# Regrouped tokens, a subtraction moved to TensorE, one pool of 21 tiles and new orders in a recurrence-and-experts kernel

## The chip, the cores and the metric

The kernel runs on one core of one Trainium2 chip. The metric is the device time of one execution in microseconds; the median of three runs of the kernel before is 293.84 us (289.77, 293.84 and 294.34). TensorE (PE) multiplies matrices, VectorE (DVE), ScalarE (ACT) and GpSimd (POOL) work elementwise, SyncE (SP) issues nearly all DMAs.

## The reference

The input is four sequences of 5056 tokens with 256 channels, 20224 tokens in all, everything fp32. First a gated linear recurrence runs along each sequence, then a soft mixture of 8 experts with 4 slots each (32 slots) runs over all tokens:

```
a_t = exp(8 * sigmoid(r) * log(sigmoid(a_param)))
h   = a_t * h + sqrt(max(1 - a_t*a_t, 1e-6)) * sigmoid(i) * x     # y[:, t] = h
logits = y @ phi                                                  # 20224 x 32
d = softmax of logits over the tokens;  slots = d.T @ y           # 32 x 256
slot_out = relu(slots @ w1[e]) @ w2[e]                            # per expert, 256 -> 1024 -> 256
out = softmax of logits over the slots @ slot_out
```

The experts need a maximum and a sum over all tokens, so no output row can be written before the last token has passed the recurrence.

## The kernel before, in words

Tokens are cut into 40 quads of 512 (the last has 256), and quads into 21 units: quad 0, then pairs of quads (1024 tokens), then quad 39. Tasks carry names: a letter code, a number (quad, unit or group) and often the half of the channels after a dot.

Per quad or unit, before the experts:

- `Dr`, `Di`, `Dx` load the three inputs (512 KB each). `TR` transposes r on PE into a two-bank tile of PSUM (tag `pair`, of which there are three), `SR` takes a tanh of it on ACT (L835) into a tile `A`, `EX` an exp (L912, two units in one instruction where their tiles are neighbours).
- `SQ` squares `A` on POOL (L896), `RT` takes the root on ACT (L931), `SI` is the gate of i on ACT (L850 or L848), `P1` (L864, L866) turns a tanh into a sigmoid, `U` multiplies gate and x on POOL (L876). A letter per unit in the string `IV` chooses the gate: P has the `P1`, E lets PE add i*x and x while it transposes (twice the transposes in `TU`, L950, no `P1`), S uses the sigmoid table.
- `TU` transposes the product into a `pair` tile (L950); on DVE `ST` (L967) multiplies it by the root there and `SC` (L984) scans it, 1024 tokens per instruction.
- `TY` (L1010) transposes the scan's result back, `YC` copies it to a tile `yn` on DVE (L1026) or ACT (L1024), in halves of 512 columns, each through half a `pair` or a single-bank tile (tag `one`, of which there are two).

Tokens are gathered into groups: 1536 tokens in the first, 2048 in the next nine, 256 in the last. Per group `LG` computes logits (L1090), `LE` copies them and takes a running maximum M on DVE (L1103), `LD` forms M minus logits on POOL (L1133; the last two groups on DVE, L1137), `TE` transposes that, `ES` takes the exp (L1157), `AC` multiplies by `yn` (L1179), `DD` and `DM` form the factor that rescales the sum (L1164, L1167), and `AE` adds on DVE (L1200). The last two groups share one maximum.

The end chain: `MT MX MR MC WJ WE W` find a maximum over the rows, `SP` contracts the sums with W (L1390), `SL` copies (L1400), `L1` and `L2` are the experts (L1439, L1487), `HZ` clears their operand on ACT (L1418), `HS`, `HT`, `HR` stand between, `SO`, `RS`, `SH` (L1503, L1505, L1508) copy, spread and copy the result. Then per group `CT CM CS CE RR CN` make the second softmax, `HP HE OT OE` (L1594, L1605, L1607, L1622, L1636, L1638) make outputs, and `OD` writes them (L1653). The weights (`w1e`, `w2e`: 16 transfers of two parts, L1342 and L1344) take freed input tiles.

Nothing chooses the order at run time: the constant `ORDER` names every task of each engine, and `run_fixed` replays it with durations only to give tiles out. PE gets spare transposes (`WU`, L1318) where that replay sees a gap. Each engine runs its own list in order and waits for what a task needs. Big tiles have tag `b`: 20 of [128, 2, 512], handed out by `take`; input tiles of one quad have tag `st`, five of them. Lines quoted here are those of the kernel before:

```
A[p - 1].mate = A[p]                 # second unit of an EX pair gets the neighbour tile
yp = Buf("pair" if q in YP4 else ONE, f"yp{q}.{b0}")      # YP4 = () before
```

Of the kernel before, what the change touches and what calls it, by code (L numbers as in the profile page):

```python
# [94 lines left out]
ORDER = {
    "PE": """
        AT TR0 TR1 TR2 TR3 TU0.1 TU0.0 TR5 TU1.0 TR6 TR4 TU1.1 TR7 TR9 TY0.0 TY2.0 TY0.2 TR10 TR8 TY1.0 LG0.0 LG0.1 TU2.0 TR11 TU2.1 TY1.2 TU3.1 TR12
        TU3.0 TR15 TY4.0 TR13 TR16 TY2.2 TR14 TY3.0 LG1.0 TY4.2 LG1.1 TU4.1 TE1 TE0 TU4.0 TR17 TR18 TU5.0 AC0.0 AC0.1 TY3.2 TU5.1 AC0.2 AC0.3 TY6.0
        TY5.0 TY8.0 TY7.0 CT1 TY8.2 TY6.2 TY5.2 AC1.0 AC1.1 AC1.2 AC1.3 TY7.2 TY9.0 TY9.2 TU6.0 TU6.1 LG2.0 TR19 LG2.1 TU7.0 TY10.0 TR21 TR22 TU7.1
        TR20 TU8.0 CT0 TR24 LG3.0 TR23 LG3.1 TY10.2 TU8.1 TR25 TR26 TE2 TY11.0 TU9.0 AC2.0 AC2.1 AC2.2 AC2.3 TE3 TY11.2 TY13.0 TU9.1 CT2 TR28 TY12.0  # L100
        TY15.0 TY14.0 TY13.2 TY14.2 TY16.0 TY12.2 TU10.1 TY16.2 TU10.0 LG4.0 AC3.0 LG4.1 TR27 AC3.1 AC3.2 AC3.3 TU11.0 TY17.0 TR29 TR30 TY18.0 TU11.1
        TY15.2 TR31 LG5.0 TU12.0 TR33 LG5.1 TU12.1 TR32 TR34 TY17.2 TU13.0 TE4 TY18.2 TU13.1 TE5 AC4.0 TY20.0 AC4.1 TR37 AC4.2 AC4.3 TY19.0 TY20.2
        TY23.0 TY24.0 TY21.0 TY22.0 TY22.2 TY19.2 TY21.2 TU14.1 LG6.0 TU14.0 LG6.1 TY23.2 TR35 TU15.0 AC5.0 AC5.1 TU15.1 AC5.2 AC5.3 TR38 TY25.0 TR36
        TY27.0 TU16.1 TY26.0 TE6 TU16.0 LG7.0 LG7.1 TU17.0 TR39 TY27.2 TY26.2 TY24.2 TY25.2 TY28.0 TU17.1 TE7 TY28.2 AC6.0 AC6.1 AC6.2 AC6.3 TY29.0
        TY29.2 TU18.1 TY31.0 TY31.2 TY30.0 TY30.2 TU18.0 LG8.0 AC7.0 AC7.1 LG8.1 AC7.2 AC7.3 TY32.0 TY33.0 TU19.0 TY34.0 TY33.2 TU19.1 TE8 TY32.2
        TY35.0 TY34.2 TY36.0 TU20.0 TY36.2 AC8.0 AC8.1 AC8.2 LG9.0 AC8.3 TU20.1 TY35.2 LG9.1 LG10.0 LG10.1 TY37.0 TY37.1 TY38.0 MT TY38.1 TE10 TE9
        TY39.0 TY39.1 MC AC9.0 AC9.1 AC9.2 AC9.3 AC10.0 CT4 SP DN L1.0 L1.1 L1.2 L1.3 L1.4 L1.5 L1.6 HT0 L1.7 L2.0 L2.1 L2.2 HT1 L2.3 L2.4 L2.5 L2.6
        L2.7 CT3 RS HP0.0 HP0.4 OT0.0 OT0.4 HP1.0 HP1.8 OT1.0 HP2.0 OT1.8 OT2.0 CT7 HP2.8 OT2.8 HP3.0 CT5 HP4.8 CT6 CT8 OT3.0 HP4.0 OT4.8 CT9 HP7.8
        HP3.8 OT4.0 CT10 OT7.8 OT3.8 HP5.8 HP6.8 HP7.0 OT5.8 OT7.0 HP6.0 HP5.0 HP8.0 OT6.0 OT6.8 OT8.0 OT5.0 HP9.0 HP9.8 HP8.8 OT9.0 OT8.8 HP10.0
        OT10.0 OT9.8  # L110
    """,
    "ACT": """
        SA LN SR0 EX0.1 EX0.0 SR1 SR2 SI0 EX1.0 EX1.1 SI1 RT0.0 RT1.0 SR3 SR5 SI3 SR6 SR4 EX2.0 SR7 SR9 EX2.1 SI5 SR8 SR10 RT2.0 RT3.0 SR11 EX4.0
        EX4.1 SR12 SI9 SR15 SI7 SR13 RT4.0 RT5.0 SR14 SR16 EX6.0 ES0 SR17 SR18 EX6.1 ES1 DM1 EX8.0 EX8.1 SI11 SI13 SI15 SI17 RT6.0 RT8.0 RT9.0 RT7.0
        SR19 SR21 SI23 SR22 SR20 DM2 EX10.0 EX10.1 SR23 SR24 SI19 SR25 SR26 ES2 YC11.0 EX12.1 EX12.0 ES3 YC11.2 SI21 YC12.0 RT10.0 YC16.0 RT12.0
        RT11.0 YC16.2 RT13.0 DM3 SR27 SR28 SI25 SR29 CE1 YC17.0 YC18.0 SR30 YC15.2 SR31 EX14.0 SR33 EX14.1 DM4 SR32 SR34 YC17.2 EX16.0 EX16.1 ES4 ES5
        SI27 SI29 RT15.0 RT14.0 RT17.0 SI31 SR35 SR37 SI33 RT16.0 SR38 SR36 YC27.0 DM5 EX18.0 EX18.1 YC26.0 ES6 SI35 YC27.2 SR39 YC26.2 YC24.2 SI37
        ES7 DM6 YC28.2 RT18.0 YC29.0 YC29.2 YC31.0 YC31.2 SQ19.1 YC30.2 YC30.0 RT19.0 CE2 YC32.0 YC33.0 DM7 EX20.0 YC34.0 SI39 EX20.1 YC33.2 ES8
        YC32.2 YC35.0 YC34.2 YC36.0 RT20.0 YC36.2 DM8 YC35.2 HZ YC37.0 YC37.1 YC38.0 YC38.1 ES9 YC39.0 ES10 WE YC39.1 DM9 CE4 HS0 HS1 CE0 HE0.0 HE0.4
        OE0.0 OE0.2 OE0.4 HE1.0 OE0.7 CE3 HE2.0 OE1.2 OE1.1 OE1.8 OE1.11 OE1.9 HE2.8 OE2.8 OE2.2 OE2.9 CE7 OE2.10 HE4.8 OE2.11 OE3.0 OE3.1 OE3.3 CE5  # L120
        CE6 OE4.8 OE4.10 HE3.8 OE4.1 OE4.2 OE4.3 OE7.8 OE7.11 OE7.10 OE7.9 OE3.9 CE9 HE5.8 CE8 OE3.11 HE7.0 OE5.8 OE5.10 HE6.8 OE5.9 OE7.3 HE6.0 OE7.1
        OE6.0 CE10 OE6.2 OE6.1 OE6.3 OE6.8 OE6.11 OE5.2 OE8.1 OE5.1 HE9.8 OE8.8 OE9.2 HE10.0 OE8.9 OE9.3 OE10.0 OE9.8 OE8.11
# [1567 lines left out]
```

## Time and profile before

| | us |
|---|---|
| median of three runs | 293.84 |
| the runs | 289.77, 293.84, 294.34 |
| span of the profiled execution, first to last instruction | 287.8 |
| fastest run, 2.0 above that span | 289.77 |
| busy: PE, ACT, DVE, POOL | 249.0, 241.4, 230.1, 195.7 |
| moved by DMA | 100.04 MB |
| written to the output | 20.71 MB |

The profile has no separate time for its own execution; the span is 2.0 us under the fastest of the three runs. Busy time is an average over stages: the recurrence lasts until about 207 us, the experts to 231 us, and from 237 us the outputs are written. The share of one stage is read from the views by window.

### The profile page before, as it was taken

To read this page: it belongs to the slowest core of one execution; us is meant where nothing else is said; L and a number is where in the kernel's file an instruction comes from. 1 tells how busy PE (TensorE), PEld (TensorE's weight loads), DVE (VectorE), ACT (ScalarE), POOL (GpSimd) and SP (SyncE) were. 2 spreads that over 40 slices of the span, in tenths; PEclk is the share of its full clock that TensorE was granted. 3 is DMA by queue.
4 is the path that set the end of the run, shared out by engine and by line. 5 is a ranking of instruction groups with operands and counts; after the bars stand their busy time and mean duration, and the time that the engine had idled before them with its cause. 6 is when DMAs were issued, how large, how long until landed. Compare 5 with 4: busy or idle time off the path is not lost.

```text
span 287.8 us, 6063 instructions
## 1 busy us (share of the span) xinstructions
PE 249.0 (87%) x2359; PEld 186.6 (65%) x2359; DVE 230.1 (80%) x280; ACT 241.4 (84%) x265; POOL 195.7 (68%) x152
## 2 busy tenths in 40 slices
...
POOL 1399997989999999999999999997102201132000
...
GB/s 280 415 408 410 401 409 410 406 409 406 408 380 232 277 381 294 317 186 223 380 412 318 364 299 369 370 370 335 360 416 361 9 110 419 416 414 416 419 410 283
DMA packets 27408, 100.04 MB, mean 348 GB/s; under 512 B 3058, under 2 KB 3060, under 8 KB 24948
## 3 DMA queue, kind: packets, MB, share of 16 engines
...
q14 instruction: 10, 0.08, 0.1%
HBM read 78.94 MB, written 20.71 MB: 346 GB/s over the span
## 4 chain that ended last, share of the span: by engine, by line
PE 29%; ACT 24%; DMA 12%; DVE 11%; POOL 11%; issue 8%; SPq 1%; DVEq 0%; ACTq 0%; POOLq 0%
DMA b<-in_i_gate_dram 7%; PE bank L1622 6%; POOL b L876 6%; ACT b L835 5%; DVE b L984 5%; ACT b L912 4%; ACT b L931 4%; PE pair L950 3%; ACT b L848 3%; PE bank L1439 3%; DMA st<-in_moe_w_dram 3%; PE bank L1487 2%; DVE pair L967 2%; DMA b<-in_x_dram 2%; ACT b L850 2%
## 5 line engine op out<-in xcount | busy, mean ns | idle before, releaser
L876 POOL TENSOR_TENSOR b<-b,b 128x1024 f32<-128x1024 f32 x36 | 84.9, 2386 | 0.2
L896 POOL TENSOR_TENSOR b<-b 128x1024 f32<-128x1024 f32 (+2 forms) x40 | 72.7, 1839 | 13.8 <-ACT b L912 10.7
L950 PE MATMUL pair<-ident,b 128*128 128x128 f32 x412 | 52.9, 276 | 7.9 <-ACT b L835 4.2
L950 PEld LDWEIGHTS pair<-ident,b 128*128 128x128 f32 x412 | 45.0, 141 | 17.8 <-POOL b L876 7.7
L967 DVE SCALAR_TENSOR_TENSOR pair<-b,pair 128x1024 f32<-128x1024 f32 (+2 forms) x42 | 48.2, 1149 | 8.2 <-PE pair L950 4.9
L984 DVE TENSOR_TENSOR_SCAN b<-b,pair 128x1024 f32<-128x1024 f32 (+6 forms) x26 | 47.6, 1845 | 0.2
L984 DVE TENSOR_TENSOR_SCAN b<-b,b,pair 128x1024 f32<-128x1024 f32 (+2 forms) x22 | 45.6, 2076 | 0.4
L824 PE MATMUL pair<-ident,st 128*128 128x128 f32 x316 | 41.8, 280 | 4.2 <-DVE b L984 1.5
L912 ACT ACTIVATE b<-b,ca 128x2048 f32<-128x2048 f32 (+3 forms) x24 | 42.2, 1798 | 0.1
L824 PEld LDWEIGHTS pair<-ident,st 128*128 128x128 f32 x316 | 35.4, 143 | 10.7 <-DVE b L984 5.1
L1557 POOL TENSOR_TENSOR b<-b,rs_all 128x512 f32<-128x512 f32 (+2 forms) x11 | 10.5, 961 | 46.1 <-DVE rs_all L1552 20.3
L835 ACT ACTIVATE b<-pair 128x1024 f32<-128x1024 f32 (+1 forms) x40 | 39.1, 1013 | 2.4 <-PE pair L824 2.3
L1010 PE MATMUL one<-ident,b 128*128 128x128 f32 x200 | 31.1, 280 | 4.0 <-ACT yn L1024 1.2
L1622 PE MATMUL bank<-hs,hT 32*128 32x256 f32 x234 | 27.8, 420 | 4.1 <-DVE hT L1607 1.9
L1010 PEld LDWEIGHTS one<-ident,b 128*128 128x128 f32 x200 | 22.0, 141 | 11.9 <-DVE yn L1026 3.8
L1636 ACT COPY b<-bank 128x512 f32<-128x512 f32 x36 | 20.0, 597 | 10.3 <-PE bank L1622 9.5
L931 ACT ACTIVATE b<-b 128x2048 f32<-128x2048 f32 (+2 forms) x15 | 25.9, 1768 | 0.1
L1622 PEld LDWEIGHTS bank<-hs,hT 32*128 32x128 f32 x234 | 18.6, 197 | 9.3 <-DVE hT L1607 3.1
L1622 PE MATMUL one<-hs,hT 32*128 32x256 f32 x82 | 21.2, 430 | 1.9 <-ACT hT L1605 1.1
L1026 DVE COPY yn<-one 128x512 f32<-128x512 f32 x29 | 19.5, 681 | 2.6 <-PE one L1010 2.6
L850 ACT ACTIVATE b<-b 128x2048 f32<-128x2048 f32 x11 | 21.1, 1921 | 0.0
L1090 PE MATMUL one<-b,phi_sb 128*32 128x512 f32 x156 | 20.9, 601 | 0.1
...
## 6 DMA issues: line engine op xcount, KB each, us to landing
...
```

The source lines that it names most:

```text
L824: nc.tensor.transpose(out=o[:, m, :], in_=raw("r", q)[:, m * D + h * P : m * D + (h + 1) * P], identity=ident,)
L835: nc.scalar.activation(dst, t(rp)[:, :, :c], AF.Sigmoid if SIGR else AF.Tanh, scale=1.0 if SIGR else 0.5)
L850: nc.scalar.activation(v, v, AF.Tanh, scale=0.5)
L876: eng.tensor_tensor(out=o, in0=a, in1=b, op=ALU.mult)
L896: eng.tensor_tensor(out=o, in0=v, in1=v, op=ALU.mult)
L912: nc.scalar.activation(v, v, AF.Exp, scale=ca[:, h : h + 1], bias=ca[:, h : h + 1])
L931: nc.scalar.activation(v, v, AF.Sqrt, bias=quarter if f != 1.0 else f, scale=-f)
L950: nc.tensor.matmul(o[:, m, :], raw(nm, q)[:, m * D + h * P : m * D + (h + 1) * P], ident, is_transpose=True, start=(nm == nms[0] and m == ...
L967: nc.vector.scalar_tensor_tensor(v, t(Nb[p])[:, h, :c], 0.5e-3 if gate_of(quads(p)[0]) == "E" else 1e-3, v, op0=ALU.max, op1=ALU.mult)
L984: nc.vector.tensor_tensor_scan(dst, dst, flat()[:, s0:s1], init, op0=ALU.mult, op1=ALU.add)
L1010: nc.tensor.transpose(out=flat()[:, b * D + h * P : b * D + (h + 1) * P], in_=tokens(q, b0 + b, 1)(h), identity=ident,)
L1622: nc.tensor.matmul(t(ops[x])[:, c * D : (c + 1) * D], t(hT)[r, off : off + (P - 1) * ns + 1 : ns], t(soRb)[r, :], start=True, stop=True,)
```

## The change

- `GROUPING` becomes "B": the first group is quad 0 alone (512 tokens), eight groups of 2048 follow, then a group of 1024 tokens in four segments of 256, and the tail of 256: twelve groups, and the two that share the last maximum hold 1280 tokens instead of 2304.
- In groups 0 to 7 `LD` on POOL goes: `TE` transposes the logits themselves, and `TF` adds the negated maximum with four more transposes into the same bank; `NM` makes the negated maximum (five on POOL, three on DVE). Groups 8 to 11 keep `LD` (8, 10 and 11 on DVE, 9 on POOL), now in `st` tiles. `DD` goes: `DM` takes M before as bias.
- `YP4` lists nearly all quads: their `TY` fills one whole `pair` tile and one `YC` copies 1024 columns. `YC` moves from 43 DVE and 37 ACT instructions to 25 and 19.
- `IV` changes from PPEEEESSSSEPPESSSSPPP to PEEEEPEESSSSEPEPSSSPS: eight units of kind E instead of six.
- One SBUF tile holds 21 `b` tiles; `EX` takes two units at any distance up to 15 tiles. The separate tiles of `lD`, `hs` and `hT` go.
- r of quad 0 is loaded, transposed and passed in halves (`TR0`, `TR0b`, `SR0`, `SR0b`). `SQ0.1` and `P10` move from DVE to POOL, `P12` goes.
- The last `AE`, `SP`, `SO`, `RS` and `SH` are cut in two halves of columns. `HZ` moves from before the last copies to between the experts' two layers on ACT.
- All five lists of `ORDER` are new.

```diff
-        groups = [[(0, o, P) for o in range(0, QT, P)]]
+        groups = [[(0, 0, QT)]]
...
-        A[p - 1].mate = A[p]
-        A[p].led = True
+        A[p].near = A[p - 1]
...
+            lo, hi = sorted(A[u].slot[0] for u in (us if len(us) == 2 else us * 2))
+            if len(us) == 2 and hi - lo > 15:
+                vs = [t(A[u])[:, h, : plen(u)] for u in us]
             else:
+                vs = [T["all"][:, H * lo + h : H * hi + h + 1 : H * (hi - lo), :] if len(us) == 2 else t(A[p])[:, h, :c]]
...
+                    nc.tensor.matmul(
+                        t(ep)[:, b * rows : (b + 1) * rows],
+                        nM[:rows, mg : mg + 1].broadcast_to([rows, P]) if part else lS(g)[:rows, b * P : (b + 1) * P],
+                        ident[:rows, :rows], is_transpose=True, start=(part == 0 and b == 0), stop=(part == 1),
+                        skip_group_check=True,
+                    )
...
+            LD[g] = add(("POOL", "DVE"), f"LD{g}", 0.1 + 0.56 * L / QT, deps=[le], prio=pos - 30 + fin, emit=e_ld,
+                        alloc=[lD], uses=[lSb[g // 4]], alt={"DVE": 0.09 + 0.36 * L / QT})
...
-                nc.gpsimd.tensor_tensor(out=dm[:rows, g : g + 1], in0=M[:rows, g - 1 : g], in1=M[:rows, g : g + 1], op=ALU.subtract)
+                    dm[:rows, g : g + 1], M[:rows, g : g + 1], AF.Exp, scale=-1.0, bias=M[:rows, g - 1 : g])
...
+        for k, c in enumerate((slice(0, P), slice(P, D + 1))):
+                nc.vector.scalar_tensor_tensor(
+                    accS[:r, c], accS[:r, c], dm[:r, mg : mg + 1], t(acc)[:r, c], op0=ALU.mult, op1=ALU.add,
...
+        a = add("PE", "SP0", 0.26, deps=[w, AE["a"]], prio=-60, alloc=[sp], emit=lambda: e_sp(0), shape="M")
+        a = add("PE", "SP1", 0.26, deps=[a, AE["b"]], prio=-60, uses=[sp], emit=lambda: e_sp(1), shape="M")
```

The tail of the new orders, after the scan of unit 19 has begun (ACT and DVE):

```
ACT  YC29.0 YC30.0 YC29.2 RT20.0 YC31.0 SQ19.1 YC32.0 RT19.0 YC34.0 ES8 CE2 YC33.0 DM8 ES9 DM9 YC35.0 YC37.0
     YC38.0 YC36.0 DM10 YC38.1 ES10 CE1 ES11 YC39.1 WE CE4 HS0 CE3 HZ HS1 SO0 HE0.0 SH0 SH1
DVE  ST18.0 LD8 SC18.0 ST18.1 SC18.1 ST19.0 LE9 SC19.0 ST19.1 AE8 SC19.1 ST20.1 SC20.1 ST20.0 SC20.0 LE10 LE11 LD11
     AE9 MX LD10 MR YC37.1 WJ YC39.0 W AE11a AE11b CM4 SL
```

## Rows read from the trace of the kernel before

**Rows 1.** Page, part 2: POOL busy tenths and DMA rate in 40 slices of the span.

```profile
POOL 1399997989999999999999999997102201132000
...
GB/s 280 415 408 410 401 409 410 406 409 406 408 380 232 277 381 294 317 186 223 380 412 318 364 299 369 370 370 335 360 416 361 9 110 419 416 414 416 419 410 283
```

**Rows 2.** Stretches: us; busy (instructions) of PE, PEld, DVE, ACT, POOL; clock; DMA share; GB/s.

```profile
40.00:80.00 40.00, 34.78 (x297) 27.94 (x299) 35.86 (x34) 39.88 (x30) 36.64 (x21) 1.00 1.03 408
...
120.00:160.00 40.00, 38.17 (x348) 28.58 (x346) 39.53 (x39) 39.88 (x35) 39.74 (x25) 1.00 0.82 310
160.00:208.00 48.00, 43.40 (x421) 30.57 (x421) 47.83 (x44) 47.62 (x58) 40.11 (x29) 1.00 0.97 354
```

**Rows 3.** DVE timeline: start us, us, instruction, count, idle before; units 2, 19, 20.

```profile
40.27 1.23 DVE L967 SCALAR_TENSOR_TENSOR pair<-b,pair 128x1024 f32<-128x1024 f32 x1 [2.47 <-ACT b L931]
...
198.01 1.23 DVE L967 SCALAR_TENSOR_TENSOR pair<-b,pair 128x1024 f32<-128x1024 f32 x1
...
206.85 0.75 DVE L984 TENSOR_TENSOR_SCAN b<-b,b,pair 128x256 f32<-128x256 f32 x1
```

**Rows 4.** DVE timeline: pairs of equal instructions back to back.

```profile
54.78 1.26 DVE L1026 COPY yn<-one 128x512 f32<-128x512 f32 x2
...
85.83 2.36 DVE L967 SCALAR_TENSOR_TENSOR pair<-b,pair 128x1024 f32<-128x1024 f32 x2 [0.83 <-ACT b L931]
88.10 4.58 DVE L984 TENSOR_TENSOR_SCAN b<-b,b,pair 128x1024 f32<-128x1024 f32 x2
```

**Rows 5.** ACT timeline: a table load, copies, two tanh, the root of unit 19.

```profile
34.99 1.93 ACT L835 ACTIVATE b<-pair 128x1024 f32<-128x1024 f32 x2
...
185.81 1.28 ACT L931 ACT_TABLE_LOAD   x1
...
189.87 1.08 ACT L1024 COPY yn<-one 128x512 f32<-128x512 f32 x2
...
192.72 1.96 ACT L931 ACTIVATE b<-b 128x2048 f32<-128x2048 f32 x1
```

**Rows 6.** Groups by form, POOL: count, then busy us, mean ns, idle before.

```profile
L1133 POOL TENSOR_SCALAR lD<-b,M 128x512 f32<-128x512 f32 x8 | 5.6, 705 | 1.3 <-DVE b L1103 1.3
...
L1164 POOL TENSOR_TENSOR dm<-M 128x1 f32<-128x1 f32 x9 | 1.8, 213 | 6.5 <-DVE b L1103 6.5
```

**Rows 7.** Timeline, start of the run: one operation twice on DVE, and POOL beside it.

```profile
11.57 0.69 DVE L864 TENSOR_SCALAR st<-st 128x1024 f32<-128x1024 f32 x1 [2.82 <-ACT st L850]
...
15.64 2.38 DVE L864 TENSOR_SCALAR b<-b 128x1024 f32<-128x1024 f32 x1
...
12.74 4.73 POOL L896 TENSOR_TENSOR b<-b 128x1024 f32<-128x1024 f32 x2 [2.81 <-ACT b L912]
```

**Rows 8.** PE timeline: sixteen transposes, and the task after them.

```profile
37.47 1.91 PE L950 MATMUL pair<-ident,b 128*128 128x128 f32 x16
39.22 0.38 PE L1318 MATMUL one<-ident 128*128 128x128 f32 x2
```

**Rows 9.** Stretches as in rows 2, PE's spare transposes alone (PE, PEld).

```profile
40.00:80.00 40.00, 1.50 (x9) 0.66 (x7) 1.00 1.03 408
```

**Rows 10.** Timelines of ACT, PE, DVE and SP in the end chain.

```profile
207.20 1.91 ACT L1418 ACTIVATE b<-ident 128x2048 f32<-128x2048 f32 x1
...
211.81 2.37 PE L1179 MATMUL bank<-yn,eS 128*32 128x257 f32 x36
...
216.05 6.25 PE L1439 MATMUL bank<-b,yn 128*32 128x256 f32 x112 [0.39 <-DVE yn L1400]
...
231.29 0.42 DVE L1503 COPY hs<-bank 128x256 f32<-128x256 f32 x1 [2.21 <-PE bank L1487]
...
212.23 1.96 SPq L1344 DMA_DIRECT2D b<-in_moe_w_dram  x4
234.66 0.36 SPq L1653 DMA_DIRECT2D out_dram<-st  x1
```

**Rows 11.** Stretch as in rows 2, while outputs are written.

```profile
250.00:270.00 20.00, 16.95 (x175) 11.66 (x179) 16.84 (x37) 14.49 (x31) 4.45 (x5) 1.00 1.01 417
```

More of the change, by code (lines that the diff above doesn't have):

```diff
@@ L111 @@
+        OT10.4 OT5.0
     """,
     "ACT": """
[L113 to L120, printed above, removed]
@@ new lines @@
+        SC10.0 SC10.1 YC18.0 CM2 ST11.1 SC11.1 LE5 ST11.0 SC11.0 CS2 ST12.1 SC12.1 ST12.0 SC12.0 ST13.0 SC13.0 AE4 ST13.1 YC19.0 SC13.1 LE6 YC20.0
+        ST14.0 ST14.1 SC14.0 SC14.1 ST15.1 SC15.1 AE5 LE7 YC25.0 ST15.0 NM6 NM7 YC23.0 SC15.0 YC24.0 ST16.1 SC16.1 ST16.0 YC26.0 SC16.0 AE6 ST17.0
+        ST17.1 SC17.0 LE8 SC17.1 AE7 ST18.0 LD8 SC18.0 ST18.1 SC18.1 ST19.0 LE9 SC19.0 ST19.1 AE8 SC19.1 ST20.1 SC20.1 ST20.0 SC20.0 LE10 LE11 LD11
+        AE9 MX LD10 MR YC37.1 WJ YC39.0 W AE11a AE11b CM4 SL RR1 CS4 RR2 CM3 CS3 RR4 HR0 HR1 RR0 RR3 RD SO1 HE1.8 OE0.0 OE0.2 OE1.8 OE1.11 OE1.2
@@ L196, in __init__ @@
         self.need, self.late = {}, None
[L198 removed]
+        self.mate = self.kept = self.near = None
         self.led = False
@@ L405, in begin @@
                 self.table = KIND[t.kind][0]
+            if t.name == "LN":
+                self.table = "exp"
             t.start, t.eng_used = now, e
@@ L523, in take @@
             free = self.slots["b"]
-            i = min(range(len(free)), key=lambda i: (free[i] ^ 1) in free)
+            by = b.near.slot[0] if b.near is not None and b.near.slot else None
+            i = min(range(len(free)), key=lambda i: (by is not None and abs(free[i] - by) > 15, (free[i] ^ 1) in free))
             b.slot = [free.pop(i)]
```

336 lines of the change are left out of this document (188 added, 148 removed).

## The prediction

> **What bounds the kernel now.** I read the span in slices first [rows 1]: from 237 us to the end the DMA rate stands at 410 to 419 GB/s, so the last 50 us are paid by bytes (20.71 MB at 417 GB/s are 49.7 us) and only their start can move. In slices 1 to 10 the rate is also above 400, later it dips to 186: input tiles are full then, and computing sets the pace. Next the stretches [rows 2]: from 40 to 208 us ACT is busy 39.88 of 40 twice and 47.62 of 48; DVE has 4.1 us idle in 40 to 80 and hardly any later; POOL is full in 120 to 160 and free for 7.9 us at the end; PE stands at 34.8 to 38.2 of 40. So the recurrence has three engines without slack, and a saving on one is worth what the other two allow. Last the timelines: unit 2's first multiply starts at 40.27 after waiting 2.47 us for ACT's root, and the last scan ends at 206.85 + 0.75 = 207.6 [rows 3]; the experts start at 216.05, the first output is issued at 234.66 [rows 10].
>
> The sum is made against the profiled execution, span 287.8. The fastest run, 289.77, is 2.0 above it; the other two lie 4 us higher, for which the profile has no reason. I add the change of span to 292.0, the middle of the three runs' spread; the median, 293.84, is 1.8 above that.
>
> **Merged copies.** I price by the distance of starts, since neighbours overlap. On DVE two half copies take 1.26 with one of 0.68 at the end, so a start every 0.58 to 0.60; a multiply of 1024 columns from the same kind of tile starts every 1.15 [rows 4]. On ACT two copies take 1.08, a start every 0.48; two tanh of 1024 columns 1.93, a start every 0.95 [rows 5]. So a full copy (estimate 1.13 to 1.15 on DVE, 0.95 on ACT) costs nearly what its halves cost: at most 0.07 us saved on DVE, 0.01 on ACT, per quad.
>
> **DVE from unit 2 to the last scan.** Before, by starts: 38 multiplies and 38 scans (1.15 and 2.27, short ones less) 125.3, 39 half copies 23.4, eight `LE` 5.8, eight `AE` 3.1, six of the second softmax 3.6, together 161.2. The stretch lasts 167.3, so 6.1 is idle. After: the same 125.3, 21 full copies 23.7, nine `LE` 6.5, nine `AE` 3.5, four of the second softmax 2.4, `LD8` 0.7, two `NM` 0.2: 162.4. DVE gains nothing: copies that it gives up in number it takes back in width, and `LE9` and `AE8` come forward from the end chain.
>
> **ACT up to the root of unit 19.** I sum the list in order, a start distance for each (tanh 0.95, gate 1.85, exp 2.03, root 1.89, table load 1.28). Against the list before, the new one has ahead of this root: one more table load (eighteen against seventeen) +1.3, both small exps and the root of unit 20 and its gate +2.2, nine full and two half copies instead of 21 halves -0.9, halves of `SR0` and one more `DM` +0.2; together +2.7. Before, the root ended at 194.68 [rows 5], now at 197.4. By the same sums the roots of units 2 and 3 end together no later, but unit 3 comes first and unit 2's root is 1.1 later.
>
> **Where the scans end.** By ACT: unit 19's multiply can start at 197.5 (before 198.01, behind other scans); from there to the last scan is 9.6 before, and 10.3 now with `LE9` between: 207.8. By DVE: 40.27 + 1.1 + 162.4 and the idle time, where I take 4.0 of the 6.1 (the new roots of units 4, 8, 10, 14 and 18 come 0.5 to 1 us after DVE is ready): 207.8. Both agree, +0.2. Bounds of the idle time are 0, as POOL's relief could give, and 10, if each wait doubles.
>
> **POOL.** Gone: eight net `LD` of 0.70, nine `DD` of 0.21 against five `NM` like them [rows 6], most of one `P1`; with the constants moved ahead of the squares, about 10 us less from `U1` to its last task. I cost this as no gain of its own, since ACT and DVE cover POOL from 40 us on; it is what could shrink the idle time above. `LD8` goes to DVE with both operands in SBUF while POOL works. The one row of this kind: the same multiply-add over 1024 columns took 0.69 on DVE while POOL stood still, and 2.38 at 15.64 while POOL ran its square until 17.46 [rows 7]. So `LD8` costs 0 to 1.7 more than its 0.7; with half the columns I take +0.8. [...] `LD10` and `LD11` meet an idle POOL.
>
> **PE.** Sixteen transposes start every 1.75 (37.47 to 39.22) [rows 8], 0.109 each. Two more units of kind E add 32 (3.5), `TF` 32 (3.5), the twelfth group about 1.3: +8.3 in 165 us. The spare transposes, which could give way, are only 1.5 in 40 to 80 [rows 9] and none after 120. I cost it at zero: the tightest stretch has 1.8 of 40 idle [rows 2] and PE runs ahead of DVE. If the cover is gone it is the second rival.
>
> **Start.** `SR0` in halves wins 0.6 at most, but `SR3` to `SR6` are put ahead of the first root and x of quad 0 is loaded twelfth instead of eighth. It is in the +1.1 above; the queue of SP is otherwise the same 512 KB transfers with one more. The 21st tile and the freed neighbours let loads start earlier; after 80 us they already wait for tiles [rows 1], so I take 0.
>
> **End chain.** Between the last scan and the experts 8.45 passed. The last joint groups need 20 instead of 36 matmuls of `AC` (2.37 us, so -1.0) [rows 10]; `LE`, `LD` and `ES` of 256 columns instead of 512 save 0.3 each, partly beside other work; `AE8` leaves. Against it `CE1` stands between `ES10` and `ES11` on ACT (0.6), `YC37.1` and `YC39.0` between the maximum's steps on DVE, and `CM4` ahead of `SL`. Following PE, DVE and ACT by these durations gives 7.0: -1.45 (bounds -2.5 and 0). `HZ`, 1.91 [rows 10], now sits between `CE3` and `HS1`; `CS3` comes about 4.3 after the experts start, so `HZ` ends at 6.9, where 6.7 was needed: +0.4. `SO`, `RS` and `SH` in halves on two engines save 0.5 of the 1.9 from the last expert matmul to the first output matmul. Weights: the last issue ended at 214.2, 12 us before its use [rows 10]; the new list puts `w14` fourteenth, needed 3.1 us after `L1` begins. I take 0, up to +3.
>
> **Outputs.** 417 GB/s in 250 to 270 with DVE at 16.84 and ACT at 14.49 of 20 [rows 11]: producers have slack; a twelfth group adds about 2 us to them, hidden by the DMA. 0, up to +1.
>
> Sum: +0.2 + 0.8 - 1.45 + 0.4 - 0.5 = **-0.5 us**, span 287.3, time 292.0 - 0.5 = **291.5**.
>
> **Rivals.** *Faster, waits dissolve.* POOL's 10 us let DVE's idle 6.1 shrink to 1 instead of 4.0 (-3), `LD8` costs nothing extra (-0.8), the first roots come no later (-1.1), the chain is at its good end (-1.1): 285.5. For it: POOL has no gap in 120 to 160 [rows 2]. Against it: ACT's order puts unit 19's root at 197.4, whatever POOL does. Chance 0.22.
>
> *Fixed price of an instruction.* By rows 4 a multiply of 1024 columns lasts 2.36 - 1.15 = 1.21 and a half copy 0.68, so 0.53 is columns and 0.15 of each instruction is not. If every instruction paid that in full, 21 merges would give 3.2 where my tally has 1.5: 289.8. [...] The rows show starts 0.58 apart, with half of the 0.15 hidden. Chance 0.08.
>
> *Slower, the three `pair` tiles.* Before, most `TY` went through a single bank or half a pair; now each holds a whole `pair` through `TY` (0.87), a hand-over of about 0.2 and a copy of 1.13: 2.2. `TR` and `SR` hold one for 2.0. DVE keeps two with the unit in scan and the next one. So the third tile serves 4.2 us per quad, and the pace is 167.3 over 36.5 quads, 4.6. With PE's 8.3 more work on top, a wait of 0.2 per quad beyond those counted is +7: 298.5. It decides from 0.16 per quad on (2%). For it: both loads stand near their limit at once. Against it: two-bank tiles are free whenever DVE copies instead of scanning. Chance 0.14. That the change does not do what it says (EX split because tiles lie too far apart, 0.3 each, a few times) stays inside the forecast.
>
> **Numbers.** Forecast, no change that shows: 0.56; the fixed price 0.08 also lies within 2% (5.9 us, about what a measurement of this kernel can tell from no change). So faster by over 2% 0.22, within 0.64, slower 0.14. The range reaches to the faster rival and a little beyond, as runs differ by 4 us, and to the slower one: 284.5 to 298.5. The forecast's own range is 288 to 296.
>
> **What would show it.** Last scan at 207 to 209.5; root of unit 19 ending at 197 to 199; full copies of 1.15 to 1.2 on DVE and 1.02 on ACT; `LD8` above 1 us; experts 6.5 to 7.5 after the last scan; outputs still at 417 GB/s. It is wrong if the last scan ends before 204 (waits dissolved), or if PE's transposes of `TR` and `TY` wait for DVE or ACT by many us more than before, with DVE idle above 10 us between 40 us and the last scan.

## The result, and the profile after

| | before | after |
|---|---|---|
| median of the runs (20 each) | 290.94 us | 292.2 us |
| span of the profiled execution | 287.8 us | 289.8 us |
| end of the last scan | 207.6 | 210.47 |
| start of the experts | 216.05 | 217.91 |
| first output issued | 234.66 | 236.56 |
| from there to the end | 53.14 | 53.24 |

The ratio is 1.0053 [1.0028, 1.0078]: some 1.5 us slower, a small loss whose interval does not hold 1, where I had forecast 0.5 us faster. The ratio leaves out the slow runs (of the kernel after the one of 295.0 us), so it is not quite the quotient of the two medians. Timed again beside the last experiments, the kernel after gave 1.0038 [1.0007, 1.0070]. By the profiles the loss is 2.0 us, and it is complete when the last scan ends: +2.9 there, -1.0 in the end chain, +0.1 in the outputs.

The page's slices answer to [rows 1]: POOL is done a slice earlier (the 28th slice has 1 for 7), and the rate at the end still stands above 400.

```profile
POOL 5475997999998699999999999991000331140000
...
GB/s 285 400 414 409 399 409 412 401 412 408 366 403 370 340 393 413 405 75 261 284 313 407 189 368 161 408 389 378 404 405 260 3 90 415 422 415 417 417 401 289
```

The stretches of [rows 2] and [rows 11], after (us; PE, PEld, DVE, ACT, POOL; clock, DMA share, GB/s). DVE and ACT stand as full as before up to 160 (ACT's 3.5 idle in the last stretch lie nearly all behind its root of unit 19), and PE is 3.2 us busier in 40 to 80:

```profile
40.00:80.00 40.00, 38.03 (x334) 30.31 (x333) 37.55 (x33) 39.88 (x30) 37.81 (x21) 1.00 1.02 400
120.00:160.00 40.00, 36.20 (x319) 28.11 (x321) 39.14 (x32) 39.55 (x32) 39.50 (x23) 0.96 0.77 280
160.00:208.00 48.00, 44.35 (x420) 31.95 (x413) 47.65 (x41) 44.54 (x46) 36.67 (x21) 1.00 0.86 324
250.00:270.00 20.00, 15.87 (x155) 10.30 (x153) 18.05 (x42) 12.01 (x25) 4.16 (x6) 1.00 1.01 417
```

DVE's timeline answers to [rows 3 and 4]: the first multiply of unit 2, a merged copy, then unit 18 with `LD8` (L1191) behind its first multiply, unit 19 and the last scan.

```profile
33.77 1.22 DVE L1064 COPY yn<-pair 128x1024 f32<-128x1024 f32 x1 [0.70 <-PE pair L1048]
34.92 2.34 DVE L1022 TENSOR_TENSOR_SCAN b<-b,pair 128x1024 f32<-128x1024 f32 x1
...
41.81 1.23 DVE L1005 SCALAR_TENSOR_TENSOR pair<-b,pair 128x1024 f32<-128x1024 f32 x1 [0.99 <-PE pair L988]
...
190.82 1.23 DVE L1005 SCALAR_TENSOR_TENSOR pair<-b,pair 128x1024 f32<-128x1024 f32 x1
191.96 2.59 DVE L1191 TENSOR_SCALAR st<-b,M 128x512 f32<-128x512 f32 x1
194.48 2.33 DVE L1022 TENSOR_TENSOR_SCAN b<-b,pair 128x1024 f32<-128x1024 f32 x1
...
200.23 1.21 DVE L1005 SCALAR_TENSOR_TENSOR pair<-b,pair 128x1024 f32<-128x1024 f32 x1
...
209.72 0.75 DVE L1022 TENSOR_TENSOR_SCAN b<-b,pair 128x256 f32<-128x256 f32 x1
...
212.92 0.33 DVE L1191 TENSOR_SCALAR st<-b,M 128x256 f32<-128x256 f32 x1
```

`LD8` takes 2.59 us for 512 columns; the same instruction with 256 columns takes 0.33 when POOL is idle. POOL's timeline beside it:

```profile
191.90 2.38 POOL L912 TENSOR_TENSOR b<-b 128x1024 f32<-128x1024 f32 x1
194.22 2.09 POOL L932 TENSOR_TENSOR b<-b 128x1024 f32<-128x1024 f32 x1
```

POOL's product ends at 194.28, `LD8` at 194.55, 0.27 later. The square behind it takes 2.09 us, where others take 1.9.

ACT and PE in the end chain, answering to [rows 5 and 10]: the root of unit 19, `HZ`, ACT's half of `SO`; the last `AC`, the experts' matmuls, the first output matmul; then DVE's side of it.

```profile
197.08 1.91 ACT L969 ACTIVATE b<-b 128x2048 f32<-128x2048 f32 x1
...
222.49 1.90 ACT L1481 ACTIVATE b<-ident 128x2048 f32<-128x2048 f32 x1
...
233.20 0.27 ACT L1569 COPY eS<-bank 128x128 f32<-128x128 f32 x1 [7.11 <-PE bank L1551]
```

```profile
214.57 1.52 PE L1226 MATMUL one<-yn,eS 128*32 128x257 f32 x20
...
217.91 1.07 PE L1503 MATMUL bank<-st,yn 128*32 128x256 f32 x16
...
225.41 1.91 PE L1551 MATMUL bank<-b 128*32 128x256 f32 x32
...
227.69 5.39 PE L1551 MATMUL bank<-b 128*32 128x256 f32 x96
...
234.91 0.48 PE L1695 MATMUL bank<-eS,yn 32*128 32x256 f32 x1 [0.36 <-ACT eS L1569]
```

```profile
224.42 0.29 DVE L1538 TENSOR_SCALAR b<-bank 128x128 f32<-128x128 f32 x1 [1.57 <-ACT b L1481]
...
233.50 0.29 DVE L1571 COPY eS<-bank 128x128 f32<-128x128 f32 x1 [2.43 <-ACT eS L1569]
```

The root ends at 198.99 (forecast 197 to 199), and the multiply that needs it starts at 200.23 with no wait: DVE is late, not ACT. The two halves of `SO` run one after the other: DVE's starts 0.03 after ACT's has ended, with ACT named as what it waited for.

### The profile page after: what moved, and what is told of

It is laid out like the page before. It is cut to its first block, busy times and chain, and to the rows that moved or that the text cites. A ratio compares the mean times of both kernels' runs of the same rounds, so it can differ in the third digit from the quotient of the medians.

```text
span 289.8 us, 6157 instructions
## 1 busy us (share of the span) xinstructions
PE 256.5 (89%) x2429; PEld 195.1 (67%) x2429; DVE 230.7 (80%) x271; ACT 240.5 (83%) x253; POOL 188.9 (65%) x141
## 5 line engine op out<-in xcount | busy, mean ns | idle before, releaser
L1022 DVE TENSOR_TENSOR_SCAN b<-b,pair 128x1024 f32<-128x1024 f32 (+8 forms) x48 | 92.9, 1952 | 0.8
L912 POOL TENSOR_TENSOR b<-b 128x1024 f32<-128x1024 f32 x38 | 89.5, 2374 | 6.2 <-ACT b L969 2.4
L988 PE MATMUL pair<-ident,b 128*128 128x128 f32 x444 | 56.3, 275 | 4.4 <-DVE yn L1064 1.9
L988 PEld LDWEIGHTS pair<-ident,b 128*128 128x128 f32 x444 | 48.6, 141 | 11.8 <-issue 2.8
L1048 PE MATMUL pair<-ident,b 128*128 128x128 f32 x288 | 38.5, 278 | 5.7 <-DVE yn L1064 2.7
L1048 PEld LDWEIGHTS pair<-ident,b 128*128 128x128 f32 x288 | 31.9, 142 | 14.9 <-ACT b L844 4.5
L1695 PE MATMUL bank<-eS,yn 32*128 32x256 f32 x238 | 29.5, 416 | 4.0 <-DVE yn L1680 2.0
L1064 DVE COPY yn<-pair 128x1024 f32<-128x1024 f32 x23 | 28.0, 1216 | 2.1 <-PE pair L1048 1.9
L1695 PEld LDWEIGHTS bank<-eS,yn 32*128 32x128 f32 x238 | 20.0, 201 | 9.1 <-ACT b L1709 2.6
L1226 PE MATMUL one<-yn,eS 128*32 128x257 f32 x316 | 23.4, 386 | 0.5 <-ACT eS L1206 0.5
L1128 PE MATMUL one<-b,phi_sb 128*32 128x512 f32 (+1 forms) x164 | 23.4, 601 | 0.0
L1695 PE MATMUL one<-eS,yn 32*128 32x256 f32 x78 | 20.7, 431 | 1.3 <-DVE yn L1680 1.3
```

The costliest lines, as they stand in the source:

```text
L912: eng.tensor_tensor(out=o, in0=a, in1=b, op=ALU.mult)
L988: nc.tensor.matmul(o[:, m, :], raw(nm, q)[:, m * D + h * P : m * D + (h + 1) * P], ident, is_transpose=True, start=(nm == nms[0] and m == ...
L1022: nc.vector.tensor_tensor_scan(dst, dst, flat()[:, s0:s1], init, op0=ALU.mult, op1=ALU.add)
L1048: nc.tensor.transpose(out=flat()[:, b * D + h * P : b * D + (h + 1) * P], in_=tokens(q, b0 + b, 1)(h), identity=ident,)
L1064: nc.vector.tensor_copy(out=dst, in_=v)
L1128: nc.tensor.matmul(t(lp)[32 * j : 32 * j + NS, :L], phi_sb[:, h, :], tokens(q, o // P, L // P)(h), start=(h == 0), stop=(h == H - 1),)
```

## The experiments

Changes of order are shown as the places in the lists of `ORDER` that differ.

### What LD8 costs

**e1_ld8_pool**: the kernel after, `LD8` on POOL.

```diff
 DVE
-ST18.0 LD8 SC18.0
+ST18.0 SC18.0
 POOL
-SQ20.1 U37
+SQ20.1 LD8 U37
```

> The changed kernel with LD8 moved from DVE to POOL, behind the squares of unit 20. Theory A (the stall of LD8 beside POOL, 2.59 us for a planned 0.45, delays every later scan): unit 18's first scan starts 2.5 us earlier after its multiply, the last scan ends at 208.0 instead of 210.5, the span falls by 2 to 2.5 us and the ratio to the kernel before is 0.996 to 0.998. Rival B (ACT's root of unit 19, which ends at 199.0, or PE sets the end and the scans would wait for it anyway): DVE gets a wait of over 1.2 us before unit 19's multiply, the last scan moves by less than 1.2 us and the ratio stays above 1.001.

Ratio to before 0.9975 [0.9944, 1.0007]. POOL's `LD8`, then DVE's `ST18.0`, `ST19.0` and last scan:

```profile
192.53 0.70 POOL L1179 TENSOR_SCALAR st<-b,M 128x512 f32<-128x512 f32 x1
```

```profile
191.42 1.23 DVE L993 SCALAR_TENSOR_TENSOR pair<-b,pair 128x1024 f32<-128x1024 f32 x1
...
199.39 1.23 DVE L993 SCALAR_TENSOR_TENSOR pair<-b,pair 128x1024 f32<-128x1024 f32 x1 [0.85 <-ACT b L957]
...
208.76 0.75 DVE L1010 TENSOR_TENSOR_SCAN b<-b,pair 128x256 f32<-128x256 f32 x1
```

I measure the price of `LD8` by the distance from the start of `ST18.0` to that of the last scan, since the start of the recurrence differs by up to 2.7 us from one execution to the next (first scan at 22.8 to 25.5 in the kernels with 21 tiles and the new start, 18.7 to 18.9 in the three with the old one): 18.90 in the kernel after (190.82 to 209.72), 17.34 here, although `ST19.0` now waits 0.85 for ACT's root. The stall was worth 1.56 us at the end. That is nearer to theory A, with part of rival B: the last scan ends 1.0 earlier (209.51), not 2.5, and the span falls by 1.0.

**e2_ld8_psum**: `LD8` stays on DVE in its place, but reads the logits from PSUM instead of from their copy in SBUF.

```diff
-eng.tensor_scalar(t(lD)[:rows, :L], lS(g)[:rows, :L], -1.0, ...
+v = t(lp) if g == LDG else lS(g)
+eng.tensor_scalar(t(lD)[:rows, :L], v[:rows, :L], -1.0, ...
```

> The changed kernel with LD8 still on DVE at the same place, but reading the logits from PSUM instead of their copy in SBUF. Theory A (what stalls is one input in SBUF and the output in SBUF in a fast form beside a POOL operation): LD8 takes 0.70 to 0.75 us while POOL works, as the same operation did before from PSUM, and the last scan ends 1.8 us earlier, near 208.7. Rival B (any write of DVE to SBUF at that place waits for POOL, or LD8 waits for its output tile): LD8 again takes over 2 us and nothing moves.

One execution, 292.0 us. DVE's timeline, then POOL's:

```profile
191.84 0.74 DVE L1192 TENSOR_SCALAR st<-one,M 128x512 f32<-128x512 f32 x1
192.51 2.34 DVE L1022 TENSOR_TENSOR_SCAN b<-b,pair 128x1024 f32<-128x1024 f32 x1
```

```profile
191.79 2.36 POOL L912 TENSOR_TENSOR b<-b 128x1024 f32<-128x1024 f32 x1
194.11 1.89 POOL L932 TENSOR_TENSOR b<-b 128x1024 f32<-128x1024 f32 x1
```

The place, the engine and POOL's work are the same; only the source differs, and 2.59 becomes 0.74. POOL's square is back at 1.89. Theory A: from `ST18.0` to the last scan 17.64. The form from SBUF to SBUF is the faster one where POOL is idle (0.69 for 1024 columns [rows 7], 0.74 here for 512 from PSUM). So it is the meeting of that form with POOL that costs, not the place.

**e5_before_ld7**: the mirror, in the kernel before: `LD7` from POOL to DVE.

```diff
 POOL
-SQ18.1 LD7 P135
+SQ18.1 P135
 DVE
-LE7 SC16.0 ST17.0
+LE7 SC16.0 LD7 ST17.0
```

> The kernel before with one thing of the change put in: LD7 leaves POOL for DVE, behind the scan SC16.0, reading and writing SBUF while POOL multiplies and squares. Theory A (LD8 cost 1.8 us more than its 0.7 because DVE in its fast form gives way to POOL): LD7 lasts 2.0 to 2.6 us on DVE, a neighbour such as the copies keeps its time, the last scan ends 1.5 to 2.5 us later than in the kernel before, and the ratio to it is 1.004 to 1.009. Theory B (the 2.59 us belonged to that place in the kernel after alone, a tile or a write queue there, and the end moved for other reasons): LD7 lasts 0.3 to 0.8 us and the ratio is 0.998 to 1.003.

A miss for theory A, with the numbers of theory B: 0.9993 [0.9951, 1.0034], and `LD7` took 0.48. But POOL's rows (count; ns min, median, max; first and last start) show that it met only two one-tensor instructions, of 1.13 and 1.29 us:

```profile
182.08 0.48 DVE L1124 TENSOR_SCALAR lD<-b,M 128x512 f32<-128x512 f32 x1
```

```profile
L853 POOL TENSOR_SCALAR b<-b,half_sb x2: 1128/1211/1294, 181.2 to 182.3; 128x1024 f32<-128x1024 f32 x2
```

The first of them, begun at 181.15, ended at 182.28; `LD7` ended at 182.56, again 0.28 later. That turned theory A into a sharper one: DVE stands still until POOL's running instruction ends. The next run puts `LD7` into the middle of a product.

**e9_before_ld7_late**:

```diff
 DVE
-SC16.0 LD7 ST17.0 YC25.2 YC28.0 ST17.1
+SC16.0 ST17.0 YC25.2 YC28.0 LD7 ST17.1
```

> As the run with LD7 of the kernel before on DVE, but LD7 stands 2.6 us later in DVE's list, behind the copy YC28.0, where POOL is inside a product of two tensors (183.5 to 185.9 us in that run) and not in the one-tensor multiply-add beside which LD7 took 0.48 us. Theory A1 (DVE's instruction from SBUF to SBUF stands still until POOL's running product of two tensors ends, and then needs 0.3 to 0.5 us): LD7 starts at about 184.7 and ends 0.25 to 0.6 us after the end of the product beside it, so it lasts 1.3 to 1.8 us; last scan 0.8 to 1.4 us later than in the kernel before. Theory A2 (it runs at a lower pace beside any work of POOL): 2.0 to 2.6 us, whatever is left of the product. Theory B (LD8 was a special case of the kernel after): 0.4 to 0.6 us.

```profile
185.02 1.61 DVE L1124 TENSOR_SCALAR lD<-b,M 128x512 f32<-128x512 f32 x1
```

```profile
L863 POOL TENSOR_TENSOR b<-b,b x2: 2368/2468/2569, 184.0 to 186.3; 128x1024 f32<-128x1024 f32 x2
```

POOL's first product ran from 183.98 for 2.37, to 186.35; `LD7` ended at 186.63, 0.28 later, and the second product took 2.57 in place of 2.37. A1 holds to the tenth; A2 and B fall. The ratio is 1.0071 [1.0032, 1.0109]: the last scan came 2.7 us later, more than the 0.8 to 1.4 expected, because `ES7` stands in ACT's order and waited 1.94 for `LD7`'s transposes, with the roots of units 18 and 19 behind it. So 1.6 us on DVE cost the end 2.7; the later place of `LD7` has its part in ACT's wait, and no run parts it from the stall.

**e12_ld8_pool_again** is e1 once more, the same kernel.

> The kernel after with LD8 on POOL behind SQ20.1 alone, run once more with more rounds: whether it beats the kernel before. Theory A (LD8's extra 1.8 us was what made the change a loss, and without it the change is a small gain): ratio to the kernel before 0.994 to 0.999 with the interval under 1. Theory B (without it the two are equal): interval holds 1.

1.0016 [0.9978, 1.0055]: theory B, equal to the kernel before. From `ST18.0` to the last scan 17.32.

### The merged copies and the halves

**e3_half_copies**: the kernel after with each merged `YC` as two copies of 512 columns (`TY` stays whole).

```diff
 (DVE and ACT, each merged quad)
-YC16.0
+YC16.0 YC16.2
```

> The changed kernel with every full copy of 1024 columns cut in two copies of 512, one behind the other on the same engine from the same two-bank tile; the transposes stay whole. Theory A (starts overlap, so a full copy costs nearly its halves): +0.07 us for each of the 22 copies on DVE in the recurrence, about +1.5 us on the last scan, and nothing on ACT; ratio to the kernel before 1.008 to 1.012. Rival B (each instruction pays its fixed 0.15 us): +3.2 us, ratio 1.015 to 1.018. Rival C (copies are not on the path): no change, ratio 1.005.

1.0083 [1.0049, 1.0116]. Groups by line, DVE: 46 half copies here, 23 full ones in the kernel after (busy us, mean ns).

```profile
L1049 DVE COPY yn<-pair 128x512 f32<-128x512 f32 x46 | 29.4, 682 | 2.1 <-PE pair L1030 1.9
```

```profile
L1064 DVE COPY yn<-pair 128x1024 f32<-128x1024 f32 x23 | 28.0, 1216 | 2.1 <-PE pair L1048 1.9
```

Two halves back to back last 1.26 to 1.29, one full copy 1.22. `ST18.0` starts at 192.57 instead of 190.82. The merge saves the 0.07 us per quad that starts gave, nothing like a fixed price of 0.15. That is theory A; the ratio alone would not tell it from rival C, the rows do.

**e4_unsplit**: `AE11`, `SO`, `RS` and `SH` of the kernel after whole again; `SP` stays in two tasks, which now both wait for the whole `AE11`.

```diff
-for k, c in enumerate((slice(0, P), slice(P, D + 1))):
+for k, c in enumerate((slice(0, D + 1),)):
...
-cols = (slice(0, D // 2), slice(D // 2, D))
+cols = (slice(0, D),)
```

> The changed kernel with the end chain whole again: AE11, SP, SO, RS and SH each in one instruction, SO on DVE and SH on ACT. Theory A (the halves of SO on two engines ran one after the other, ACT 233.20 to 233.47 and DVE from 233.50, so halving hid nothing there, and AE and SP in halves hid 0.3 at most): first output matmul 1.8 to 1.9 us after the last expert matmul as now, experts start 0 to 0.3 us later, span +0.0 to +0.4, ratio 1.004 to 1.007. Rival B (the halves save what was forecast, 0.5 us or more at the result alone): 2.3 us or more from the last expert matmul to the first output matmul, ratio over 1.007.

1.0048 [1.0011, 1.0086], as the kernel after: theory A. From the end of the last expert matmul (229.12 + 5.39) to the first output matmul, at 236.27, 1.76, against 1.83 with halves; from the last scan to the experts 7.55 against 7.44.

```profile
229.12 5.39 PE L1521 MATMUL bank<-b 128*32 128x256 f32 x96
```

So the halves of `SO`, `RS` and `SH` save nothing, and those of `AE11` and `SP` no more than the scatter: with halves the experts start 7.37 to 7.59 after the last scan.

### The 21st tile and the added transposes

**e7_tiles20**: `N_B = 21` becomes `N_B = 20` in the kernel after, nothing else.

> The kernel after with 20 instead of 21 tiles of tag b, all else the same. Theory A (my zero: loads after 80 us wait for tiles, but the engines never wait for a load): last scan and median within 0.5 us of the kernel after, ratio to the kernel before 1.003 to 1.008. Theory B (the 21st tile pays): the first loads or units wait, last scan 1 to 4 us later, ratio 1.009 to 1.02. It is also the reference for the kernel with LD back, which has 20 tiles.

1.0425 [1.0367, 1.0482]; the last scan ends at 222.46, 12.0 later than in the kernel after. The stretch to hold against 280 GB/s and 39.14 of DVE above, then two of the waits of 20 to 220 us (us in all, times, longest):

```profile
120.00:160.00 40.00, 36.52 (x316) 29.22 (x317) 36.91 (x33) 37.20 (x29) 37.37 (x22) 0.96 0.55 202
```

```profile
DVE pair L1005 <- PE pair L988: 17.0, 11, 6.0
...
POOL b L912 <- DMA b<-in_x_dram: 5.9, 1, 5.9
```

Loads wait for a tile (the queue's waits for `TU`'s transposes, L988, come to 37.6 from 20 to 200 us, the longest 10.9; 22.9 and 6.3 in the kernel after), POOL's product waits for x (5.9, until 178.90), PE for the product (1.1), DVE for PE (6.0, until 185.62; 17.0 in all against 4.6 in the kernel after). Theory B, and far beyond its upper end.

**e6_ld_back** (20 tiles) and **e10_ld_back21** (21 tiles): `LD` back on POOL in groups 0 to 7, `NM` and `TF` gone.

```diff
-LDG = 8
+LDG = 0
```

> The kernel after with its main part undone: in groups 0 to 7 LD is back on POOL (0.70 each, 5.6 in all, in place of five NM of 0.15) and the added transposes TF (32 of 0.109, 3.5 us of PE) and the NM go; two small tiles take the place of the 21st tile. Theory A (as in my sum: POOL and PE are both covered by ACT and DVE): last scan within 0.7 us of the kernel after, ratio to the kernel before 1.002 to 1.009. Theory B (POOL's relief is worth something): POOL's busy share in 120 to 160 stays full, DVE and ACT wait for it, last scan 1.5 to 5 us later, ratio 1.011 to 1.022. Theory C (the added transposes hold PE up): last scan 1 to 3 us earlier, ratio 0.995 to 1.001.

> The kernel after with 21 tiles, and LD back on POOL in groups 0 to 7 in place of NM and TF; the difference goes into a tile of eS, so no 4 KB are needed. LD7 stands behind U32. Theory A (POOL and PE are covered): last scan within 0.7 us of the kernel after, ratio to the kernel before 1.002 to 1.009; then the 10 us between the two runs with 20 tiles belong to the lack of tiles. Theory B (POOL's 4.9 us more delay what DVE and ACT need): last scan 2 to 8 us later, ratio 1.012 to 1.035. Theory C (the transposes cost more than the relief): ratio 0.995 to 1.001.

1.0775 [1.0706, 1.0844] and 1.0259 [1.0204, 1.0315]. Neither prices the transposes: in e10 my places for `LD6` and `LD0` made POOL wait 3.4 and DVE 2.6 us, in e6 7.3 and 2.6, and e6 also lacks the tile. But `LD8` on DVE, in e10, is the strongest row of the study. DVE, then POOL:

```profile
194.93 5.61 DVE L1168 TENSOR_SCALAR st<-b,M 128x512 f32<-128x512 f32 x1
```

```profile
194.92 1.18 POOL L908 TENSOR_TENSOR b<-b 128x256 f32<-128x256 f32 x2
196.07 2.35 POOL L888 TENSOR_TENSOR b<-b 128x1024 f32<-128x1024 f32 x1
198.38 1.89 POOL L908 TENSOR_TENSOR b<-b 128x1024 f32<-128x1024 f32 x1
```

Four POOL instructions follow each other without a gap, and `LD8` ends 0.27 us after the last of them (200.54 and 200.27). Three began while it stood waiting. In the kernel after it got in ahead of POOL's next instruction; what decides that, no run shows.

**e13_ld_back_clean**: e10 with `LD6` behind `SQ15.1`, `CT0` behind `TY3.0`, `CM0` and `CS0` behind `YC3.0`, and the tail of e11 (below).

> The run with LD back on POOL and 21 tiles, without what blurred it: LD6 stands behind SQ15.1, CT0 behind TY3.0 and CM0 and CS0 behind YC3.0, LD8 is on POOL behind SQ19.0 and the squares of unit 20, and the root of unit 20 behind that of unit 19. It is to be compared with the tail-order run (1.0005), which differs by NM and TF in place of LD. Theory A (as in my sum: POOL's 4.9 us are covered): last scan 208 to 210, ratio to the kernel before 0.998 to 1.005. Theory B (POOL's relief is worth something in 40 to 200 us): ACT waits for POOL's squares and PE for POOL's products by 2 us and more beyond the tail-order run, last scan 211 to 214, ratio 1.008 to 1.02.

1.0059 [1.0027, 1.0091], last scan ending at 210.35; e11, which differs in these parts, gave 1.0005 and 208.34. It lies just above the range of A and below that of B. From the start of `ST2.0` to the end of the last scan it takes 169.1 us, e11 167.6 and e14 (below) 167.4, and DVE idles 5.9 of that against 4.5 and 4.1. The ratio is 0.0056 above that of e14, which was timed with it. So `NM` and `TF` in place of `LD` are worth some 1.6 us here, between 0.3 and 3 by the intervals of the two ratios; the places of `CT0`, `CM0` and `CS0` differ too, and no run parts the two.

### Looking for a version that beats both

**e8_order**: `LD8` on POOL, the root of unit 20 behind that of unit 19, and an earlier start. **e11_tail_order**: the same without the start. **e14_tail_order2**: e11 with `TE8` behind `LG9.1`. **e15_after_again**: the kernel after.

```diff
 POOL
-U38 SQ20.0 SQ20.1 U37 SQ19.0 LD9
+U38 U37 SQ19.0 SQ20.0 SQ20.1 LD8 LD9
 ACT
-RT20.0 YC31.0 SQ19.1 YC32.0 RT19.0
+YC31.0 SQ19.1 YC32.0 RT19.0 RT20.0
 PE   (e8, e11; e14 has LG9.0 LG9.1 TE8)
-TE8 TY32.0 TU19.0 TY34.0 LG9.0
+TY32.0 TU19.0 TY34.0 TE8 LG9.0
 ACT, PE, DVE   (e8 alone)
-RT3.0 RT2.0 ... TE0 CT0 TU2.0 ... CM0 CS0 ST2.0 SC2.0
+RT2.0 RT3.0 ... TU2.0 TE0 CT0 ... ST2.0 SC2.0 CM0 CS0
```

> The kernel after with LD8 on POOL, and three moves that the traces suggest: on POOL the squares of unit 20 and LD8 stand behind SQ19.0; on ACT the root of unit 20 stands behind that of unit 19; at the start the root of unit 2 comes ahead of that of unit 3, TU2.0 on PE ahead of TE0 and CT0, and CM0 and CS0 on DVE behind SC2.0. Theory A (DVE's list sets the end): ST2.0 starts at 40.8 instead of 41.8 and the whole of DVE's list moves, ST19.0 starts at 198.0 to 198.8, last scan ends at 207.8 to 208.8, ratio to the kernel before 0.990 to 0.996. Theory B (ACT's list sets the end from 42 us on): the early start is lost in waits for roots by 90 us, only the swap of the roots of units 19 and 20 pays (0.6 us against the kernel with LD8 on POOL alone), last scan 208.8 to 209.4, ratio 0.994 to 0.998.

> The kernel after with LD8 on POOL behind SQ19.0 and the squares of unit 20, and the root of unit 20 behind that of unit 19; the start is left as it is in the kernel after. Theory A (the tail of ACT's list sets the end): ST19.0 starts 0.5 to 0.7 us earlier than with LD8 on POOL alone (199.39), last scan ends at 208.8 to 209.2, ratio to the kernel before 0.993 to 0.998. Theory B (something else takes its place, such as LE9 waiting for its logits behind TE8 on PE): no earlier than 209.4, ratio 0.997 to 1.003.

> The tail-order run with TE8 behind LG9.1 on PE, so that LE9 does not wait for its logits (0.43 us there). Theory A (DVE after ST19.0 is the path): last scan 0.4 us earlier than there relative to ST19.0 (9.91 from the start of ST19.0 to the start of the last scan, becomes 9.5), ratio to the kernel before 0.995 to 1.001, and to the kernel after 0.990 to 0.998. Theory B (ES8, now later, holds AC8 and AE8): the 0.4 us come back as a wait of AE8, ratio 0.999 to 1.004.

> The kernel after once more, beside the two others, for a comparison in one call: LD8 again 2.3 to 2.8 us on DVE, from the start of ST18.0 to the start of the last scan 18.7 to 19.1 us (17.3 to 17.7 in all runs where LD8 does not stall), ratio to the kernel before 1.002 to 1.008.

| run | ratio to before | `ST18.0` to last scan, us | last scan ends |
|---|---|---|---|
| after | 1.0053 [1.0028, 1.0078] | 18.90 | 210.47 |
| e15, the same | 1.0038 [1.0007, 1.0070] | 18.88 | 210.51 |
| e1 | 0.9975 [0.9944, 1.0007] | 17.34 | 209.51 |
| e12, the same | 1.0016 [0.9978, 1.0055] | 17.32 | 207.98 |
| e8 | 1.0028 [0.9991, 1.0065] | 17.58 | 208.97 |
| e11 | 1.0005 [0.9975, 1.0035] | 17.58 | 208.34 |
| e14 | 1.0003 [0.9972, 1.0034] | 17.42 | 209.27 |

In e15 `LD8` took 2.58 again. The five runs without the stall average 1.0005, the two of the kernel after 1.0046: the stall is 0.4%, some 1.2 us of median. One pair would not show it, as e1 and e12, the same kernel, differ by as much. The rows are closer: from the start of `ST18.0` to the start of the experts it takes 27.1 us in the two with the stall, 25.4 to 25.8 in the five without, and 25.7 in the kernel before.

e8's earlier start is to be held against e11, whose execution began alike (first scan at 22.77 and 22.79): unit 2's first scan at 41.51 for 42.02, but its second multiply at 45.07 for 45.05. ACT's tanh and the second multiply in e8, then the same two in e11:

```profile
41.89 1.94 ACT L811 ACTIVATE b<-pair 128x1024 f32<-128x1024 f32 x2
...
45.07 1.23 DVE L972 SCALAR_TENSOR_TENSOR pair<-b,pair 128x1024 f32<-128x1024 f32 x1 [0.71 <-PE pair L955]
...
41.87 1.94 ACT L811 ACTIVATE b<-pair 128x1024 f32<-128x1024 f32 x2
...
45.05 1.23 DVE L972 SCALAR_TENSOR_TENSOR pair<-b,pair 128x1024 f32<-128x1024 f32 x1 [0.68 <-PE pair L955]
```

The start was lost at once: DVE waited for PE's transposes and these for the first of ACT's tanh, which came at the same time in both. So ACT's list sets the pace there, as in theory B, though by a tanh and not a root, and e8's ratio lies above that theory's. In e11 `ST19.0` came 7.67 after `ST18.0`, 7.97 in e1, but `LE9` then waited 0.43 for its logits, so it is half theory A and half B (its ratio is B's); in e14 that wait is gone and 0.24 of it is back in front of `AE8` (from `ST19.0` to the last scan 9.74, 9.91 in e11). No version beats the kernel before by more than can be measured.

## Why the prediction was wrong

The time lay in the range, at 292.2 for 291.5, but the sign was wrong: +1.5 us by the runs, +2.0 by the spans, for -0.5. By the spans the steps miss by +1.0 (`LD8`), +0.9 (the scans' end), +0.5 (the halves), +0.5 (the end chain), -0.4 (`HZ`) and +0.1 (outputs), together the 2.5 between -0.5 and +2.0. `LD8` is the largest and alone turns the sign: with its +1.8 the sum is +0.5. That 291.5 lies so near 292.2 is luck: a base that was 1.1 too high (292.0 for 290.94) hides that much of the miss. Step by step, against the spans:

- **`LD8`, the step that failed.** I had +0.8, between 0 and 1.7, "with half the columns". It cost 1.8 more than its tally (2.52 from start to start, 0.7 in the sum), and e1 and e2 got 1.56 and 1.26 of it back. The row was the right one [rows 7], and read wrongly: that instruction of 1024 columns ended at 18.02, POOL's at 17.47. Its price was what was left of POOL's instruction, which no count of columns shortens. Fewer columns shorten only what follows, 0.55 there and 0.27 here. By that reading a product of POOL begun just before (2.37 each, e9) would have given up to 2.37 + 0.27 - 0.7 = +1.9 for this step, and +0.6 in all.
- **Halves of `SO`, `RS`, `SH`.** Forecast -0.5, measured 0.05 (1.83 for 1.88 before), and e4's whole ones do as well. I had let two engines read the halves side by side; they ran in turn (ACT from 233.20 to 233.47, DVE from 233.50), with ACT's copy into the same tile named as what DVE waited for.
- **End chain.** Forecast -1.45, measured -1.0 (7.44 for 8.45). The last `AC` takes 1.52 for 20 matmuls instead of 2.37 for 36, which is most of it, though no run takes that alone; the halves of `AE11` and `SP` show no gain (e4). And the gain was no gain of the whole: `LE9` and `AE8`, which left the chain, now stand ahead of the last scan, so that without the stall `ST18.0` to the experts takes what it took before (25.4 to 25.8 for 25.7).
- **`HZ`.** Forecast +0.4, measured 0: `HR0` did wait 1.57 for it, but the second layer began at 225.41, 0.7 after `HR0`, and from the first expert matmul to the last's end 15.17 passed as before.
- **Scans' end.** Forecast +0.2 apart from `LD8`, measured +1.1 (2.9 less 1.8). The start came 1.5 later, not 1.1, with `TU2.0` behind `TE0` and `CT0` on PE; in the executions with this start it lay between +0.5 and +3.1 (unit 2's first scan at 42.02 to 44.68, 41.53 before). DVE's work came to 163.6 without the stall (165.4 less 1.8) for my 162.4, and its idle time to 3.2 for my 4.0 (5.8 before). The stretches from `ST2.0` to the last scan, before and after, as in [rows 2]:

```profile
40.27:207.60 167.33, 150.93 (x1362) 112.76 (x1360) 161.53 (x152) 166.26 (x151) 155.58 (x94) 1.00 0.91 345
...
41.81:210.47 168.66, 156.11 (x1417) 118.38 (x1418) 165.42 (x138) 163.76 (x137) 148.41 (x82) 0.99 0.91 347
```

- **Merged copies, the fixed price.** Right: 1.22 per copy, 1.15 from start to start (33.77 to 34.92), and e3 shows 0.07 per pair. That rival is dead.
- **The `pair` tiles.** Not seen: PE's longest wait for DVE at `TY` was 2.5, and DVE's waits for PE's `pair` tiles stayed near those of before (4.6 and 4.9 from 20 to 210 us). The hand-over of about 0.2 was an estimate: where DVE waited for PE, it began 0.03 to 0.13 after PE's last matmul in the kernel before.
- **POOL.** "No gain of its own" was a little low: e13 puts it at some 1.6 us, waits of DVE that come back with `LD`. The faster rival fell all the same: the last scan did not end before 204.
- **The 21st tile.** "I take 0" fits only the change as a whole. Taken out of the kernel after it costs 12 us (e7): the new orders are built on it. What it would be worth with orders made for 20 tiles, no run shows.
- **The base.** 292.0 was high: the kernel before has had medians of 290.4 to 291.3 since.

Why the kernel after, with the stall gone and a chain 1.0 shorter, only equals the kernel before, the rows show in part. From `ST18.0` to the experts nothing is gained, as said. From `ST2.0` to `ST18.0` the kernels without the stall take 148.4 to 150.4 us for 150.1, and `ST2.0` starts at 40.24 to 42.28 for 40.27, so what the new lists save there a later start takes back. e8 undid the late start and gained nothing by it. Why the start differs so much between executions stays open.
